# Chunked attention and two feed-forward layers: the attention products cut into 64x64 blocks, and the order of the opening changed

## The chip, the core and the metric

The kernel runs on one core of one Trainium2 chip. The metric is the device time of one execution in microseconds (us). The engines are named as the profile names them: PE (TensorE, matrix products), PEld (its weight loads), DVE (VectorE), ACT (ScalarE), POOL (GpSimd) and SP (SyncE, which only issues transfers here).

## What is computed

```python
# q, k, v: (4, 8, 576, 64); nine chunks of 64 positions for each head
scores = scale * np.matmul(q_c, k_c.transpose(0, 1, 2, 4, 3))     # 64x64 for each chunk and head
scores = scores - np.max(scores, axis=-1, keepdims=True)
attn = np.exp(scores)
attn = attn / (np.sum(attn, axis=-1, keepdims=True) + 1e-09)
out = np.matmul(attn, v_c)                                        # 64x64 for each chunk and head
...
x = out as (2304 tokens, 512)
h = x @ w_in;  r = np.maximum(h, 0.0);  x = (s * (r * r) + b) @ w_out      # 512 -> 2048 -> 512
...
P = exp(x @ w_gate - max), then 8 rounds of row and column scaling (8 experts)
out = sum over e of P[:, e:e+1] * (np.maximum(x @ w1[e], 0.0) @ w2[e])     # 512 -> 1024 -> 512
```

The weights w_in and w_out come as 64-bit floats and are turned into 32-bit numbers on the chip.

## The kernel before

The 2304 tokens are 18 token tiles of 128, that is, two chunks of 64 (c = 0, 1), and six groups `g` of three tiles. A tile `t` holds 8 heads as four pairs `p`; h or j is the head in its pair.

**Attention**, `attn_stages(t)`, is a generator of five stages. Stage 0 transposes q and k on PE into the banks pq and pk (L252, L258), and ACT copies them out: q into qT (L254), k into a block-diagonal tile kbd with zeros beside it (L261, two instructions of 64 partitions). Stage 1 makes the scores: for each pair and chunk one product of 128 rows with 64 weight columns (qT) and 128 moving columns (kbd) into the bank sc (L272); DVE takes the row maximum (L280) and subtracts it (L282). Stage 2 is the exponential on ACT (L285), the row sums on DVE (L287 to L289) and the division on POOL (L290). Stage 3 transposes the result into pa (L295) and ACT copies it to aT (L297). Stage 4 multiplies with v: one product for each pair and chunk, 128 weight columns from the block-diagonal tile vbd, 64 moving columns of aT, into the bank px (L303). ACT rounds px into xTh (L311), DVE writes the rest into xTl (L312). The zeros of kbd and vbd are written once, at the start, by DVE (L889) and POOL (L891). A product of 32-bit floats is two records each of weight load and matmul in the trace; a transpose and a product of split operands is one.

**Order.** Nothing is scheduled by a tool: each engine runs its instructions in the order in which the code records them, and waits at the head of its queue. `attention()` yields the stages of all tiles in a skewed order, and `stage(n)` runs the next n of these steps. One tile is four steps.

**The first feed-forward layer** goes over eight units `u` of 256 hidden columns. For a unit and a group, `up1` makes two banks ph of 12 matmuls each (L107 under `three`, both operands split in a high and a low part); ACT and DVE make the hidden tiles gh (L358, L360, L364), and `later()` makes their low part gl (L339, L344). `down1` makes four banks po of six matmuls each from gh and gl of both halves, and adds them to `xacc` (L389, L391). In unit 0 the steps of the attention lie between these (`side`). `down1` of a group is recorded after `up1` of the next one, through `prev`.

**Weights.** A unit's w_in and w_out are four blocks of 512 KB (raw). `convert` and `finish` make the high part wh and the low part wl of a block with ACT (L189, L190, L213), DVE (L191 to L197, L208) and POOL (L200, L201, L214); `unit_conversion` is a generator that does them one after the other, and `next(cg)` runs its next step. Blocks 0 and 1 are the two halves of w_in, 2 and 3 those of w_out.

**The experts.** The products of the second layer go through `up_chain` and `down_chain` (all PE work at L611), each on three or four of the PSUM banks that `kept["abc"]` names in turn. In the change from the last `up_chain` to the first `down_chain`, `prep_w2_first` splits the first w2 blocks: `w2_split` is an ACT instruction (L714) and a DVE one (L715), `w2_combine` a DVE subtraction (L718).

Of the kernel before, what the change touches and what calls it, by code (L numbers as in the profile page):

```python
# [25 lines left out]
def chunk_attention_ffn_moe(ctx, tc, q, k, v, w_in, w_out, s, b, w_gate, w1, w2, out):  # L26
# [52 lines left out]
    def accumulator(n, name):  # L79
# [4 lines left out]
    kbd = [  # L84
        cv.tile([P, NP, 2, 2, CH], F32, name="kbd"),
        cv.tile([P, NP, 2, 2, CH], F32, name="kbd1"),
    ]
    vbd = [cv.tile([P, NP, 2, 2, D], F32, name=f"vbd{i}") for i in range(2)]

    qk = {(nm, 0): at.tile([P, H, D], F32, name=f"{nm}0", bufs=1) for nm in "qk"}  # L90
    for i, key in enumerate((("q", 1), ("k", 1), ("q", 2), ("k", 2))):
        c0 = i % 2 * H * D
        qk[key] = spares[4 + i // 2][:, c0:c0 + H * D].rearrange("t (h d) -> t h d", h=H)
    prs = [at.tile([P, H, CH], F32, name="pr", bufs=1)]
    for i in (4, 5):
        prs.append(spares[i][:, 2 * H * CH:3 * H * CH].rearrange("x (h k) -> x h k", h=H))
# [30 lines left out]
    def load_v(t):  # L127
        for c in range(2):
            bb, s0 = divmod(t * P + c * CH, S)
            for j in range(2):  # L130
                nc.sync.dma_start(
                    out=vbd[t % 2][j * CH:(j + 1) * CH, :, c, j, :],
                    in_=v[bb, :, s0:s0 + CH, :].rearrange(
                        "(p two) s d -> two s p d", two=2
                    )[j],
                )
# [104 lines left out]
    def attn_stages(t):  # L241
# [4 lines left out]
        vb = vbd[t % 2]  # L246
        kb = kbd[t % 2]
# [11 lines left out]
        for j in range(2):  # L259
# [18 lines left out]
        sc3 = sc.rearrange("t (h k) -> t h k", h=H)  # L278
        mx = at.tile([P, H, 1], F32, tag="mx", name=f"mx{t}")
        nc.vector.tensor_reduce(out=mx, in_=sc3, axis=AX.X, op=ALU.max)  # L280
        pr = prs[t % 3]
        nc.vector.tensor_tensor(out=pr, in0=sc3, in1=mx.to_broadcast([P, H, CH]), op=ALU.subtract)  # L282
# [17 lines left out]
        px = bank(f"px{t}")  # L300
        for p in range(NP):
            for c in range(2):
                nc.tensor.matmul(  # L303
                    px[:, p * P + c * CH:p * P + (c + 1) * CH],
                    lhsT=vb[:, p, c].rearrange("x j d -> x (j d)"),
                    rhs=aT[:, p, c * CH:(c + 1) * CH],
                    start=True, stop=True,
                )
        px3 = px.rearrange("x (p t) -> x p t", p=NP)
        xh, xl = [x[:, :, o * P:(o + 1) * P] for x in xT[g]]  # L310
        nc.scalar.activation(out=xh, in_=px3, func=AF.Copy)  # L311
        nc.vector.tensor_tensor(out=xl, in0=px3, in1=xh.bitcast(F32), op=ALU.subtract)  # L312
        if t + 2 < NTT:
            load_v(t + 2)
# [413 lines left out]
    def prep_w2_first(room):  # L728
# [16 lines left out]
        for f, (b11, b22, b12, b21) in zip(HALVES, raw):  # L745
            w2_split(0, 0, b11, f)
            yield
            w2_split(0, 3, b21, f)
            w2_combine(b11, b11, b12)
            yield  # L750
            w2_split(0, 4, b22, f)
            w2_combine(b22, b22, b11)
            yield
            w2_split(0, 1, b22, f)
            yield
            w2_split(0, 2, b11, f)
            w2_combine(b21, b21, b11)
            w2late.extend([(0, 5, b12, f), (0, 6, b21, f)])
            yield
# [124 lines left out]
    with tc.manual_schedule():  # L884
# [3 lines left out]
        for z in kbd:  # L888
            nc.vector.memset(z, 0.0)  # L889
        for z in vbd:  # L890
            nc.gpsimd.memset(z, 0.0)  # L891
# [44 lines left out]
        for u in range(NU1):  # L936
# [9 lines left out]
            for g in range(NG):  # L946
# [10 lines left out]
                hs = up1(u, g, side if u else lambda: stage(3))  # L957
                if u == 0 and g == 0:
                    for _ in cg:
                        pass  # L960
                    plan_unit(1)
                    cg = unit_conversion(4)
                    next(cg)
                elif u == 0 or g:
                    next(cg, None)
# [187 lines left out]
```

## Time and profile before

| | |
|---|---|
| time, median of 3 runs | 1969.03 us (1967.58 to 1971.49) |
| the profiled execution's own time | 1969.52 us |
| its span, first to last instruction | 1967.7 us |
| PE busy | 1933.7 us (98% of the span) |
| DVE busy | 1374.4 us (70%) |
| ACT busy | 993.6 us (50%) |
| POOL busy | 158.1 us (8%) |
| mean granted clock of TensorE | 0.996 of full speed |

Busy time is the time in which an engine had an instruction under way. PE's instructions are pipelined and their ends are modelled, so a busy PE may still wait between two of them. A change can shorten the span only where it shortens what the last engine waits for at that place.

### The profile page before, as it was taken

Reading aid. Unit: us, or ns where it says so; the run is one execution under the profiler, and the core shown is the slowest. Engines: PE = TensorE matmul, PEld = TensorE weight load, DVE = VectorE, ACT = ScalarE, POOL = GpSimd, SP = SyncE. Lnnn points to the kernel's source line nnn. Section 1 sums busy time; section 2 is a strip of 40 time slices with the busy share of each in tenths; the row PEclk is TensorE's granted clock in tenths of the full one; section 3 lists DMA queues with packets and bytes.
Section 4 is the critical chain, followed back from the end, with each engine's and each line's share of the span. In section 5 each row is a group of like instructions: output and inputs, shape, how many; then the busy total and the mean of one; then the engine's idle time right before and its main releaser. Section 6 shows DMA issues by size and latency. Waiting matters only on the chain.

```text
span 1967.7 us, 33548 instructions
## 1 busy us (share of the span) xinstructions
PE 1933.7 (98%) x13283; PEld 1911.3 (97%) x13283; DVE 1374.4 (70%) x2365; ACT 993.6 (50%) x1793; POOL 158.1 (8%) x128
## 2 busy tenths in 40 slices
PE   7999999999899999999999999999999999999999
PEld 6899999999799999999999999999999999999998
DVE  5656777775767666656565656888887878788775
ACT  5664333335544445444444444555555555555553
POOL 4333333330000000000000000000000000000000
PEclk9999999999999999999999999999999999999999
DMA  8521111100155565556555656867676766767675
GB/s 201 133 65 44 44 43 43 43 22 11 39 201 213 196 228 219 208 202 227 218 210 202 225 218 232 287 184 225 177 229 188 223 201 208 220 190 227 180 228 167
DMA packets 295726, 335.64 MB, mean 171 GB/s; under 512 B 65937, under 2 KB 254353, under 8 KB 295569
## 3 DMA queue, kind: packets, MB, share of 16 engines
q1 hardware_dynamic: 295568, 333.50, 52.2%
q8 instruction: 104, 1.70, 0.3%
q14 instruction: 54, 0.43, 0.1%
HBM read 196.63 MB, written 136.84 MB: 169 GB/s over the span
## 4 chain that ended last, share of the span: by engine, by line
PE 92%; ACT 3%; DVE 3%; issue 1%; POOL 0%; DMA 0%; SPq 0%; DVEq 0%; ACTq 0%; POOLq 0%
PE wb L611 71%; PE po L107 10%; PE ph L107 9%; PE px L303 1%; PE sc L272 1%; ACT kbd L261 0%; ACT whole L659 0%; PE pa L295 0%; DVE x L520 0%; ACT r L368 0%; DMA raw<-in_moe_w_in_dram 0%; ACT r L358 0%; DVE sm L287 0%; DVE xs L523 0%; ACT qT L254 0%
## 5 line engine op out<-in xcount | busy, mean ns | idle before, releaser
L611 PE MATMUL wb<-x,x 128*128 128x256 f32 x6048 | 727.2, 283 | 2.3 <-DVE whole L665 1.4
L611 PEld LDWEIGHTS wb<-x,x 128*128 128x128 f32 x6048 | 726.3, 192 | 3.2 <-DVE whole L665 1.6
L611 PE MATMUL wb<-x,w1h 128*128 128x384 f32 x2688 | 687.8, 337 | 6.9 <-ACT wb L686 3.2
L611 PEld LDWEIGHTS wb<-x,w1h 128*128 128x128 f32 x2688 | 485.5, 188 | 9.8 <-ACT wb L686 4.2
L611 PE MATMUL wb<-x,w1l 128*128 128x384 f32 x1344 | 452.3, 337 | 0.1
L816 DVE TENSOR_TENSOR x<-st,x 128x1024 fp32r<-128x1024 f32 (+1 forms) x288 | 308.0, 1088 | 101.5 <-ACT x L815 100.5
L815 ACT ACTIVATE x<-st 128x1024 fp32r<-128x1024 f32 (+1 forms) x288 | 272.1, 945 | 109.6 <-issue 74.4
L611 PEld LDWEIGHTS wb<-x,w1l 128*128 128x128 f32 x1344 | 253.2, 188 | 0.4 <-DVE w1l L573 0.4
L843 DVE SCALAR_TENSOR_TENSOR whole<-wb,lg,whole 128x256 f32<-128x256 f32 (+1 forms) x333 | 165.9, 529 | 49.7 <-PE wb L611 47.2
L849 ACT ACTIVATE wb<-wb 128x256 f32<-128x256 f32 x216 | 79.4, 368 | 232.3 <-PE wb L611 221.7
L674 DVE SCALAR_TENSOR_TENSOR whole<-wb,whole 128x384 f32<-128x384 f32 x192 | 98.0, 552 | 126.9 <-PE wb L611 105.5
L659 ACT ACTIVATE whole<-whole 128x384 f32<-128x384 f32 x192 | 100.3, 527 | 157.1 <-DVE whole L665 119.4
L107 PE MATMUL po<-gh,wh 128*128 128x384 f32 x384 | 130.1, 339 | 0.0
L107 PE MATMUL ph<-xTh,wh 128*128 128x384 f32 x384 | 129.0, 336 | 0.7 <-ACT xTh L311 0.7
L107 PE MATMUL ph<-xTl,wh 128*128 128x384 f32 x384 | 128.4, 334 | 0.3 <-DVE xTl L312 0.3
L107 PE MATMUL po<-gh,wl 128*128 128x384 f32 x384 | 128.4, 334 | 0.0
L107 PE MATMUL po<-gl,wh 128*128 128x384 f32 x384 | 128.4, 334 | 0.0
L107 PE MATMUL ph<-xTh,wl 128*128 128x384 f32 x384 | 128.3, 334 | 0.0
L360 DVE SCALAR_TENSOR_TENSOR r<-r,s_bc 128x384 f32<-128x384 f32 x84 | 65.9, 785 | 70.7 <-ACT r L358 70.7
L573 DVE TENSOR_TENSOR w1l<-w,w1h 128x512 fp32r<-128x512 f32 (+1 forms) x128 | 78.9, 619 | 34.3 <-ACT w1h L571 34.3
L691 ACT ACTIVATE whole<-wb 128x384 f32<-128x384 f32 x96 | 47.4, 494 | 93.9 <-PE wb L611 93.8
L364 ACT ACTIVATE gh<-r,b_bc 128x384 fp32r<-128x384 f32 x84 | 51.8, 617 | 84.3 <-DVE r L360 84.3
(135 smaller groups left out, 2022.9 us busy)
## 6 DMA issues: line engine op xcount, KB each, us to landing
h<-whole SPq DMA_DIRECT2D x96, 1344.0 KB, 5.0
st<-h SPq DMA_DIRECT2D x216, 512.0 KB, 4.2
w<-in_moe_w_dram SPq DMA_DIRECT2D x60, 512.0 KB, 6.8
st<-h SPq DMA_DIRECT2D x72, 256.0 KB, 4.2
raw<-in_moe_w_in_dram SPq DMA_DIRECT2D x16, 512.0 KB, 3.7
raw<-in_moe_w_out_dram SPq DMA_DIRECT2D x14, 512.0 KB, 3.5
vbd<-in_v_dram SPq DMA_DIRECT2D x72, 64.0 KB, 2.5
out_dram<-whole SPq DMA_DIRECT2D x18, 256.0 KB, 3.3
```

Of the source, the lines that this page charges most:

```text
L107: nc.tensor.matmul(out, lhsT=x, rhs=y, start=(i == 0), stop=(i == n - 1))
L360: nc.vector.scalar_tensor_tensor(out=r, in0=r, scalar=s_bc[:, 0:1], in1=r, op0=ALU.mult, op1=ALU.mult)
L364: nc.scalar.activation(out=hh, in_=r, func=AF.Identity, bias=b_bc[:, 0:1])
L573: nc.vector.tensor_tensor(out=dst(lo), in0=src, in1=dst(hi).bitcast(F32), op=ALU.subtract)
L611: nc.tensor.matmul(out, lhsT=x, rhs=y, start=fresh and i == 0, stop=i == n - 1, skip_group_check=True)
L659: nc.scalar.activation(out=dst, in_=src, func=AF.Relu)
L674: nc.vector.scalar_tensor_tensor(out=dst, in0=view(b), scalar=0.0, in1=y, op0=ALU.max, op1=op)
L691: nc.scalar.activation(out=u2, in_=b, func=AF.Copy)
L815: nc.scalar.activation(out=h, in_=src, func=AF.Copy)
L816: nc.vector.tensor_tensor(out=l, in0=src, in1=h.bitcast(F32), op=ALU.subtract)
L843: nc.vector.scalar_tensor_tensor(out=dst, in0=src, scalar=g, in1=dst, op0=ALU.mult, op1=ALU.add)
L849: nc.scalar.activation(out=dst, in_=src, func=AF.Copy)
```

## The change

- **Blocks.** kbd and vbd and their zeros are gone. k is copied whole into kT by one ACT instruction; v is loaded into `vs` (three buffers instead of two, loaded three tiles ahead instead of two). Each product of a pair and chunk is now two products of 64 rows, 64 weight columns and 64 moving columns, one for each head; the scores go into two banks sc_0 and sc_1, and the output of stage 4 into two banks px_0 and px_1. `head(s, c)` sets which head goes where: two products that follow each other take different row halves and different column halves of the array. Maximum, subtraction, rounding and rest are done for each of the two banks, so they are twice as many instructions of half the size.
- **Unit 0.** `down1` of a group follows `up1` of the same group for groups 0 to 4; the steps of the attention between them are written out (`steps`, 12 to a group), and `next(cg)` is called within group 0.
- **Opening.** q, k of tiles 0 to 2 and v of tile 0 are loaded ahead of the first raw block, and the first `next(cg)` comes later in the opening loop.
- **Experts.** In `prep_w2_first` the split of b22 (slot 1) changes places with that of b11 (slot 2) and a combination. In `down_banks` banks 6 and 7 change places.
- The buffers for q, k and the exponentials leave the accumulator of group 4.

```diff
-    kbd = [
-        cv.tile([P, NP, 2, 2, CH], F32, name="kbd"),
-        cv.tile([P, NP, 2, 2, CH], F32, name="kbd1"),
-    ]
-    vbd = [cv.tile([P, NP, 2, 2, D], F32, name=f"vbd{i}") for i in range(2)]
+    vs = [cv.tile([P, NP, 2, D], F32, name=f"vs{i}") for i in range(3)]
+
+    def head(s, c):
+        return s if c == 0 else 1 - s
...
-        for j in range(2):
-            h = slice(j * D, (j + 1) * D)
-            nc.scalar.activation(
-                out=kb[h, :, :, j, :],
-                in_=pk[h].rearrange("x (p c t) -> x p c t", p=NP, c=2), func=AF.Copy,
-            )
+        kT = at.tile([P, NP, P], F32, tag="kT", name=f"kT{t}")
+        nc.scalar.activation(out=kT.rearrange("x p t -> x (p t)"), in_=pk, func=AF.Copy)
...
-        sc = bank(f"sc{t}")
+        sc = [bank(f"sc{t}_{s}")[:, :NP * CH] for s in range(2)]
         for p in range(NP):
-            for c in range(2):
-                nc.tensor.matmul(
-                    sc[c * CH:(c + 1) * CH, p * P:(p + 1) * P],
-                    lhsT=qT[:, p, c * CH:(c + 1) * CH],
-                    rhs=kb[:, p, c].rearrange("x j t -> x (j t)"),
-                    start=True, stop=True,
-                )
+            for s in range(2):
+                for c in range(2):
+                    h = slice(head(s, c) * D, (head(s, c) + 1) * D)
+                    k = slice(c * CH, (c + 1) * CH)
+                    nc.tensor.matmul(
+                        sc[s][k, p * CH:(p + 1) * CH], lhsT=qT[h, p, k], rhs=kT[h, p, k],
+                        start=True, stop=True,
+                    )
...
-        px = bank(f"px{t}")
+        px = [bank(f"px{t}_{c}")[:, :NP * CH] for c in range(2)]
         for p in range(NP):
             for c in range(2):
...
+                for s in range(2):
+                    r = slice(s * CH, (s + 1) * CH)
+                    nc.tensor.matmul(
+                        px[c][head(s, c) * D:(head(s, c) + 1) * D, p * CH:(p + 1) * CH],
+                        lhsT=vb[r, p, c, :], rhs=aT[r, p, c * CH:(c + 1) * CH],
+                        start=True, stop=True,
+                    )
+        for c in range(2):
+            px3 = px[c].rearrange("x (p t) -> x p t", p=NP)
...
-        kept["abc"] = itertools.cycle([(0, 2, 5, 6), (1, 3, 4, 7)])
+        kept["abc"] = itertools.cycle([(0, 2, 5, 7), (1, 3, 4, 6)])
...
-            w2_split(0, 1, b22, f)
-            yield
             w2_split(0, 2, b11, f)
             w2_combine(b21, b21, b11)
+            yield
+            w2_split(0, 1, b22, f)
...
         plan_unit(0)
-        load_raw(0)
         load_qk(1)
-        load_raw(1)
         load_v(0)
         load_qk(2)
+        load_raw(0)
+        load_v(1)
+        load_raw(1)
+        load_v(2)
         load_raw(2)
         load_raw(3)
-        load_v(1)
...
-            if i in (0,2,4,7,10,13,16,18):
+            if i in (4, 7, 8, 10, 11, 13):
...
+                    steps = iter((2, 1, 0, 2, 2, 2, 2, 1))
+
+                    def side():
+                        stage(next(steps, 2))
+                        if g == 0:
+                            next(cg, None)
+
+                hs = up1(u, g, side)
+                if u == 0 and g < NG - 1:
+                    stage(next(steps))
+                    later()
+                    stage(next(steps))
+                    down1(u, g, hs, side)
...
```

The change moves instructions at three places that matter below. The first is the start of ACT's queue. Before, the first two instructions work on a raw weight block:

```order
L189 ACTIVATE m_182<-raw_156 128x512
L190 ACTIVATE l_184<-raw_156 128x512
L254 ACTIVATE qT_199<-pq_194 128x512
L261 ACTIVATE kbd<-pk_201 64x8x64 x2
L254 ACTIVATE qT_215<-pq_210 128x512
L261 ACTIVATE kbd_109<-pk_217 64x8x64 x2
L189 ACTIVATE m_228<-raw_160 128x512
L190 ACTIVATE l_230<-raw_160 128x512
L285 ACTIVATE pr<-pr 128x512
```

Now ACT starts with q and k, and the first exponential stands ahead of both raw blocks:

```order
L251 ACTIVATE qT_191<-pq_186 128x512
L257 ACTIVATE kT_198<-pk_193 128x512
L251 ACTIVATE qT_207<-pq_202 128x512
L257 ACTIVATE kT_214<-pk_209 128x512
L282 ACTIVATE pr_115<-pr_115 128x512
L251 ACTIVATE qT_254<-pq_249 128x512
L257 ACTIVATE kT_261<-pk_256 128x512
L187 ACTIVATE m_265<-raw_162 128x512
L188 ACTIVATE l_267<-raw_162 128x512
L282 ACTIVATE pr_116<-pr_116 128x512
```

The weight work has moved behind three tiles' stage 0 and one exponential; nothing else stands ahead of it.

The second place is ACT's queue in unit 0 after the second hidden tile of group 0 (r_0_1 and gh_0_1; 0_1 is group 0, half 1). Before:

```order
L358 ACTIVATE r_0_1_548<-ph_0_1_533 128x384
L364 ACTIVATE gh_0_1_546<-r_0_1_548,b_bc 128x384
L297 ACTIVATE aT_558<-pa_553 128x512
L254 ACTIVATE qT_565<-pq_560 128x512
L261 ACTIVATE kbd_109<-pk_567 64x8x64 x2
L285 ACTIVATE whole<-whole 128x512
L213 ACTIVATE wh_154<-whole 128x512 x2
L297 ACTIVATE aT_611<-pa_606 128x512
L311 ACTIVATE xTh_349<-px_613 128x4x128
```

Now:

```order
L357 ACTIVATE r_0_1_623<-ph_0_1_608 128x384
L363 ACTIVATE gh_0_1_621<-r_0_1_623,b_bc 128x384
L282 ACTIVATE pr_116<-pr_116 128x512
L211 ACTIVATE wh_152<-whole 128x512
L294 ACTIVATE aT_666<-pa_661 128x512
L251 ACTIVATE qT_673<-pq_668 128x512
L257 ACTIVATE kT_680<-pk_675 128x512
L388 ACTIVATE whole<-po_0_0_684 128x384
L282 ACTIVATE whole<-whole 128x512
L294 ACTIVATE aT_726<-pa_721 128x512
L388 ACTIVATE whole<-po_0_1_728 128x384
```

The eviction of po of group 0 (L388) follows the hidden tile with five rows between them; before, the whole second group of attention tiles and `up1` of group 1 lay between.

The third place is DVE's queue near the end of the `up_chain` work, within `prep_w2_first` (x1_0 to x1_2 are the split operands, whole holds b11 to b21). Before:

```order
L715 TENSOR_TENSOR x1_2_5040<-whole_107,x1_0_5038 128x512
L718 TENSOR_TENSOR whole_107<-whole_107 128x512
L715 TENSOR_TENSOR x1_1_5039<-whole_107,x1_0_5038 128x512
L674 SCALAR_TENSOR_TENSOR whole_107<-wb2_5306,whole_107 128x3x128 x2
L676 TENSOR_TENSOR whole_107<-whole_107 128x3x128
L677 TENSOR_TENSOR whole_107<-whole_107 128x3x128
L715 TENSOR_TENSOR x1_2_5040<-whole_107,x1_0_5038 128x512
L718 TENSOR_TENSOR whole_107<-whole_107 128x512
```

Now:

```order
L714 TENSOR_TENSOR x1_2_5434<-whole_107,x1_0_5432 128x512
L717 TENSOR_TENSOR whole_107<-whole_107 128x512
L714 TENSOR_TENSOR x1_2_5434<-whole_107,x1_0_5432 128x512
L717 TENSOR_TENSOR whole_107<-whole_107 128x512
L673 SCALAR_TENSOR_TENSOR whole_107<-wb2_5700,whole_107 128x3x128 x2
L675 TENSOR_TENSOR whole_107<-whole_107 128x3x128
L676 TENSOR_TENSOR whole_107<-whole_107 128x3x128
L714 TENSOR_TENSOR x1_1_5433<-whole_107,x1_0_5432 128x512 x2
```

The split that follows the first combination is now of b11 (into x1_2), which that combination doesn't write; the split of b22 (into x1_1), which it writes, comes four instructions later.

## Rows read from the trace of the kernel before

**Rows 1.** The page: shares of the chain that ended last, by engine.

```profile
PE 92%; ACT 3%; DVE 3%; issue 1%; POOL 0%; DMA 0%; SPq 0%; DVEq 0%; ACTq 0%; POOLq 0%
```

**Rows 2.** By stretch: length, then PE, PEld, DVE, ACT, POOL busy; clock, DMA.

```profile
0.00:35.30 35.30, 23.38 (x173) 19.60 (x173) 19.43 (x36) 19.89 (x34) 18.28 (x26) 0.90 0.84 195
35.30:66.00 30.70, 27.20 (x217) 23.96 (x216) 17.56 (x36) 20.00 (x37) 10.17 (x10) 0.89 0.71 170
66.00:150.45 84.45, 83.43 (x674) 79.94 (x672) 52.27 (x94) 55.94 (x106) 26.11 (x22) 1.00 0.36 89
150.45:470.00 319.55, 319.55 (x1845) 319.55 (x1845) 221.58 (x392) 129.13 (x240) 103.54 (x72) 1.00 0.12 39
...
1220.00:1225.00 5.00, 5.00 (x22) 5.00 (x21) 3.65 (x8) 1.81 (x4) 0.00 (x0) 0.66 0.48 191
```

**Rows 3.** The chain that ended last, by time: start, us, what.

```profile
107.75 1.73 PE px L303 x16
109.48 0.44 PE pq L252 x4
...
110.36 1.02 PE sc L272 x16
111.38 1.25 PE po L107 x6
...
150.61 4.16 PE ph L107 x24
```

**Rows 4.** Groups of instructions, 35.3 to 150.44, with counts and mean ns.

```profile
L303 PE MATMUL px<-aT,vbd 128*128 128x64 f32 x240 | 29.1, 274 | 2.2 <-ACT aT L297 2.2
L107 PE MATMUL ph<-xTh,wh 128*128 128x384 f32 x48 | 16.8, 350 | 0.7 <-ACT xTh L311 0.7
L272 PE MATMUL sc<-kbd,qT 128*64 128x128 f32 x224 | 16.7, 295 | 0.0
...
L107 PE MATMUL po<-gh,wh 128*128 128x384 f32 x40 | 14.2, 356 | 0.0
...
L261 ACT ACTIVATE kbd<-pk 64x512 f32<-64x512 f32 x28 | 16.5, 588 | 0.3
L312 DVE TENSOR_TENSOR xTl<-px,xTh 128x512 fp32r<-128x512 f32 x15 | 10.3, 687 | 9.0 <-ACT xTh L311 9.0
L360 DVE SCALAR_TENSOR_TENSOR r<-r,s_bc 128x384 f32<-128x384 f32 x12 | 10.0, 831 | 18.1 <-ACT r L358 18.1
```

**Rows 5.** The page's groups: narrower instructions on PSUM banks.

```profile
L849 ACT ACTIVATE wb<-wb 128x256 f32<-128x256 f32 x216 | 79.4, 368 | 232.3 <-PE wb L611 221.7
L674 DVE SCALAR_TENSOR_TENSOR whole<-wb,whole 128x384 f32<-128x384 f32 x192 | 98.0, 552 | 126.9 <-PE wb L611 105.5
```

**Rows 6.** The opening by time, one engine after another: start, us, what.

```profile
7.22 0.66 ACT L189 ACTIVATE m<-raw 128x512 f32<-128x512 f32 x1 [5.21 <-DMA raw<-in_moe_w_in_dram]
...
9.44 1.27 POOL L200 TENSOR_TENSOR l<-l,e 128x512 f32<-128x512 f32 x1 [5.26 <-ACT kbd L261]
...
27.06 1.50 POOL L290 TENSOR_TENSOR whole<-whole,sm 128x512 f32<-128x512 f32 x1
...
5.11 1.12 PE L258 MATMUL pk<-ident,k 128*128 128x128 f32 x4
...
18.55 1.09 PE L295 MATMUL pa<-ident,pr 128*128 128x128 f32 x4 [2.83 <-POOL pr L290]
...
35.30 0.42 PE L107 MATMUL ph<-xTh,wh 128*128 128x384 f32 x1
```

**Rows 7.** From `up_chain` to `down_chain` by time, ACT and PE.

```profile
1218.38 0.63 ACT L714 ACTIVATE x<-whole 128x512 fp32r<-128x512 f32 x1 [1.49 <-DVE whole L718]
...
1219.44 0.62 PE L611 MATMUL wb<-x,w1h 128*128 128x384 f32 x2 [1.78 <-ACT wb L686]
1236.37 1.69 PE L611 MATMUL wb<-x,x 128*128 128x256 f32 x12 [1.36 <-DVE whole L665]
1242.45 3.77 PE L611 MATMUL wb<-x,x 128*128 128x256 f32 x28 [0.47 <-ACT wb L849]
```

More of the change, by code (lines that the diff above doesn't have):

```diff
@@ L83, in chunk_attention_ffn_moe @@
     spares = [accumulator(max(GT), f"spare{i}") for i in range(GT.count(max(GT)))]
-    kbd = [
-        cv.tile([P, NP, 2, 2, CH], F32, name="kbd"),
-        cv.tile([P, NP, 2, 2, CH], F32, name="kbd1"),
-    ]
-    vbd = [cv.tile([P, NP, 2, 2, D], F32, name=f"vbd{i}") for i in range(2)]
[L90 to L96, printed above, removed]
+    vs = [cv.tile([P, NP, 2, D], F32, name=f"vs{i}") for i in range(3)]
+    def head(s, c):
+        return s if c == 0 else 1 - s
+    qk = {(nm, i): at.tile([P, H, D], F32, name=f"{nm}{i}", bufs=1) for i in range(2) for nm in "qk"}
+    for i, nm in enumerate("qk"):
+        qk[nm, 2] = spares[5][:, i * H * D:(i + 1) * H * D].rearrange("t (h d) -> t h d", h=H)
+    prs = [at.tile([P, H, CH], F32, name=f"pr{i}", bufs=1) for i in range(2)]
+    prs.append(spares[5][:, 2 * H * CH:].rearrange("x (h k) -> x h k", h=H))
     def bank(name):
@@ L129, in load_v @@
             bb, s0 = divmod(t * P + c * CH, S)
-            for j in range(2):
+            for h in range(2):
                 nc.sync.dma_start(
-                    out=vbd[t % 2][j * CH:(j + 1) * CH, :, c, j, :],
+                    out=vs[t % 3][h * CH:(h + 1) * CH, :, c, :],
                     in_=v[bb, :, s0:s0 + CH, :].rearrange(
                         "(p two) s d -> two s p d", two=2
-                    )[j],
+                    )[head(h, c)],
                 )
@@ L245, in attn_stages @@
             xT[g] = new_x(g)
-        vb = vbd[t % 2]
-        kb = kbd[t % 2]
+        vb = vs[t % 3]
         a = qt.pop(t)
@@ L267, in attn_stages @@
         yield
-        sc = bank(f"sc{t}")
+        sc = [bank(f"sc{t}_{s}")[:, :NP * CH] for s in range(2)]
         for p in range(NP):
-            for c in range(2):
-                nc.tensor.matmul(
-                    sc[c * CH:(c + 1) * CH, p * P:(p + 1) * P],
-                    lhsT=qT[:, p, c * CH:(c + 1) * CH],
-                    rhs=kb[:, p, c].rearrange("x j t -> x (j t)"),
-                    start=True, stop=True,
-                )
-        sc3 = sc.rearrange("t (h k) -> t h k", h=H)
-        mx = at.tile([P, H, 1], F32, tag="mx", name=f"mx{t}")
-        nc.vector.tensor_reduce(out=mx, in_=sc3, axis=AX.X, op=ALU.max)
-        pr = prs[t % 3]
-        nc.vector.tensor_tensor(out=pr, in0=sc3, in1=mx.to_broadcast([P, H, CH]), op=ALU.subtract)
+            for s in range(2):
[6 more added lines that the diff above has]
+                    )
+        mx = at.tile([P, 2, NP, 1], F32, tag="mx", name=f"mx{t}")
+        pr = prs[t % 3]
+        for s in range(2):
+            sc3 = sc[s].rearrange("t (p k) -> t p k", p=NP)
+            nc.vector.tensor_reduce(out=mx[:, s], in_=sc3, axis=AX.X, op=ALU.max)
+            nc.vector.tensor_tensor(
+                out=pr[:, s::2], in0=sc3, in1=mx[:, s].to_broadcast([P, NP, CH]), op=ALU.subtract)
         yield
@@ L298, in attn_stages @@
         yield
-        px = bank(f"px{t}")
+        px = [bank(f"px{t}_{c}")[:, :NP * CH] for c in range(2)]
         for p in range(NP):
             for c in range(2):
[L303 to L314, printed above, removed]
+                for s in range(2):
+                    r = slice(s * CH, (s + 1) * CH)
[6 more added lines that the diff above has]
+            px3 = px[c].rearrange("x (p t) -> x p t", p=NP)
+            xh, xl = [x[:, :, o * P + c * CH:o * P + (c + 1) * CH] for x in xT[g]]
+            nc.scalar.activation(out=xh, in_=px3, func=AF.Copy)
+            nc.vector.tensor_tensor(out=xl, in0=px3, in1=xh.bitcast(F32), op=ALU.subtract)
+        if t + 3 < NTT:
+            load_v(t + 3)
         yield
@@ L956, in chunk_attention_ffn_moe @@
                     next(cg, None)
[L957 to L964, printed above, removed]
+                if u == 0:
+                    steps = iter((2, 1, 0, 2, 2, 2, 2, 1))
[9 more added lines that the diff above has]
+                    down1(u, g, hs, side)
+                    if g == 0:
+                        for _ in cg:
+                            pass
+                        plan_unit(1)
+                        cg = unit_conversion(4)
+                    else:
+                        next(cg, None)
+                    continue
+                if u == 0 or g:
                     next(cg, None)
```

5 lines of the change are left out of this document (removed).

## Prediction, made before the changed kernel was run

> **What bounds the kernel now.** I first read the chain of work that ended last: 92% of it is PE [rows 1]. The table of stretches shows where PE does not fill its time [rows 2]. From 150.45 us, where unit 1 begins, to 470 it is busy for the whole stretch; the change leaves that work alone, so what is won or lost before 150.45 moves it as a block. In the first 35.3 us PE is busy for 23.4, at a granted clock of 0.90 (part of the time at 1.2 instead of 2.4 GHz), and nobody else is full: this is a chain of dependent steps. From 35.3 to 66 it still has gaps, at a clock of 0.89. From 66 to 150.45 it is busy for 83.4 of 84.5: there PE's own work is the bound.
>
> How much of it is work? From 35.3 on the groups hold 48 matmuls of each of the three terms of ph and 40 of po [rows 4], 264 in all, at 4.16/24 = 0.173 us [rows 3]: 45.8 us. 240 records of px (15 tiles) at 1.73 us a tile are 26.0; 224 of sc (14 tiles) at 1.02 are 14.3; some 159 transposes (13 tiles' q and k, 15 tiles' pa, four to 0.44 us) are 17.5. Together 103.6 of 115.15 us. The other 11.5 are waits and the slow clock: 0.11 of 30.7, that is 3.4 us, is the clock.
>
> **The products in blocks.** A product of px is two records, 16 a tile in 1.73 us, 0.108 each; its 64 moving columns are half of those of a transpose, which takes 0.11 a record [rows 3]. So px is not held by the moving columns but by loading 128 weight columns. The records of sc have 64 weight columns and 128 moving ones, and 16 of them take 1.02: 0.064 each, or 0.128 for two. Their mean duration is 0.295, so they overlap; the two chunks of sc lie in different column halves. After the change a tile has 32 records in sc and 32 in px, each with half the weights of px and half the moving columns of sc: 0.054 to 0.064 each if nothing overlaps, which is 1.73 to 2.04 for 32. No record before uses half of the rows, so overlap between row halves isn't shown. The bounds are no overlap (about 1.9), two at a time as in sc (16 pairs at 0.064, 1.02) and four at a time (0.5). I take two at a time, since sc is the nearest row. Beside sc there is also a price for changing the tiling: six matmuls of po take 1.25 behind it instead of 6 x 0.173 = 1.04 [rows 3]. Now px changes it too; between nothing and these 0.2 I add 0.1, the middle.
>
> So sc stays at 1.02 and px goes from 1.73 to 1.12: 0.61 for each of the 15 tiles after 35.3 is **-9.2 us**. The three tiles before are in the chain of the opening.
>
> The Trainium skill (TensorEngine Tiling (Array Packing), Tiling Modes, Key Properties) says that the tiles load weights and multiply independently, which would give four at a time. Its section Restrictions and Gotchas speaks against that: different row tiles can't use the same PSUM bank at once. The two blocks that stand next to each other in one bank differ in their row half, so by that rule only neighbours from different banks would overlap, and two at a time is what remains. By the first the sum would be that of the rival with four at a time (1941), by the second it stays at 1949. No trace here has row tiles.
>
> **The instructions around them.** ACT loses one of two L261 (0.588) [rows 4] and has two xTh of 128x256 instead of one of 128x512, 2 x 0.37 [rows 5] for about 0.59: -0.44 a tile. DVE has three instructions in halves. From 0.552 for 384 columns [rows 5] and 0.687 for 512 [rows 4], about 0.42 for 256: 0.15 more for each, 0.45 a tile. In the stretch from 66 DVE was busy for 52.3 of 84.5 and ACT for 55.9 [rows 2]; with some ten tiles there they have 56.8 and 51.5, in about 70 us: 81% and 74%. I cost this at nothing, hidden behind PE. If PE's work fell to 57 us there, DVE would be the bound and all of it would show.
>
> **The opening.** ACT's first two rows wait 5.21 us for a raw block, until 7.22, and qT starts only behind them, some 1.1 later, though pk of tile 0 ended at 6.23 and pq before it [rows 6]. The weight work of two blocks stands ahead of the first maximum on DVE. POOL's first division lets PE's pa start at 18.55. After the change the first raw block comes behind three tiles' q and k and tile 0's v. I work it out from the durations that the same instructions have in this opening: qT and kT by 7.0, sc at the slow clock (about 2, as before) to 9, four DVE halves (1.6) to 10.6, exponential 0.63, sums 1.1, division 1.3: pa at 13.7 instead of 18.55, 4.9 earlier. From there to the first ph took 16.75 us. What moves into this stretch is the weight work: POOL now does the two products of both blocks (four at 1.27), one low part and two divisions before tile 2's pa, 8.6 us after 13.7, that is 22.3. Before, tile 2's division began at 27.06 and ph followed 8.2 later [rows 6], so ph could come at 29 or somewhat before. The first raw block lands late, at about 12, an estimate (seven loads of 0.26 MB ahead of its 0.52, at the stretch's 195 GB/s [rows 2]), when ACT asks for it after three tiles of q and k. I take 29.3 for 35.30: **-6 us**, between -3 (the raw blocks hold ACT) and -9.
>
> **Unit 0.** 24 matmuls of po, 4.2 us, move forward to group 0, into the stretch from 35.3 to 66 where PE waited. Against that, po now needs the hidden tiles just made: relu 0.5, L360 0.83, gh 0.6, low part 0.6 to 0.75, about 2.6 us after ph, and the queues of ACT and DVE. Between them PE has three steps of attention (about 0.9 each) and the first four matmuls of po (0.7): 3.4 us. That covers it in a quiet group. In group 0 the low part of w_out stands on POOL behind a division that waits for an exponential, some 3 us that are not covered. Of 11.5 us of loss I expect 9.5: **-2 us**, from +6 to -5. A group also takes 27 banks instead of 21 from eight; at 18 us a group a bank is asked for again after 5.3 us, longer than evictions of two instructions take.
>
> **Experts.** At 1219.44 PE had waited 1.78 us for L686, which stood on ACT behind a split that waited 1.49 for a combination [rows 7]. The exchanged split doesn't wait for it. After this wait the clock is 0.66 from 1220 to 1225 [rows 2], 1.7 us. Both gone, less a rest of 0.4: 3.1. The exchanged banks take away the wait of 1.36 for L665 at 1236.37, but ACT's queue is full to the wait at 1242.45, so PE would wait there instead: nothing. **-3 us**, between 0 and -5.
>
> **Sum.** -9.2 - 6 - 2 - 3 = -20.2 against the profiled execution's own 1969.5: 1949.3. The median is 0.5 lower than that execution, and I predict **1949 us**.
>
> **Rivals.** *Four blocks at a time* (chance 0.27): sc and px take 0.5 less, 14.5 us. From 66 on PE would need less than DVE's 57 us, so DVE holds about half of it: -8 more, 1941. For it: sc's columns already overlap. Against it: no row. The independent tiles of the Trainium skill's page TensorEngine Tiling (Array Packing) would come out here.
>
> *Waits in unit 0* (0.15): each of the five groups stalls 2 to 3 us at po or on banks, 10 to 15 us in all: 1959 to 1964. For it: DVE's L360 waited 18.1 us for ACT in 12 times [rows 4], so the way from ph to gh is slow. Against it: from 66 on PE waits for next to nothing with ACT and DVE at 66% and 62%.
>
> *No overlap of blocks* (0.10), the one on the other side: 32 records at 0.06 take 1.9 instead of 1.02 and, with 0.1, 2.0 instead of 1.73: 14 x 0.9 + 15 x 0.27 = +16.6 instead of -9.2. The sum is then +5.6: 1975, slower. It decides from 0.054 us a record up, where the other gains are used up.
>
> *The opening and the experts give nothing* (0.05): the raw blocks hold ACT as before, and DVE holds PE at 1236: about 1958. The remaining 0.03 is for anything worse.
>
> **How the numbers follow.** Two at a time, as forecast, has 0.40; with its terms' bounds it lies between 1943 and 1957. The range from 1936 to 1966 leaves out no overlap (0.10), the rest (0.03) and the best ends of four at a time (0.05). A difference of 0.2% (4 us) is about what a measurement of this kernel can tell from no change. Faster by more than that: 0.40 + 0.27 + 0.15 + 0.05, less 0.03 for stalls that eat all, 0.84. Within: 0.05. Slower: 0.11.
>
> **What would show it.** Right: 32 records of px in about 1.1 us and of sc in about 1.0, pa of tile 0 before 15 us, the first ph at 28 to 31, the first ph of unit 1 at 133 instead of 150.45, no wait of PE for L686 in the change to `down_chain` and a clock of 1.00 there. Wrong: blocks that start one after the other at 0.054 or more; waits of PE for gl or wl at the first po of a group; DVE above 95% from 66 on.

## The result, and the profile after

The changed kernel takes 1987.0 us (median of 4 runs, 1985.62 to 1988.73), beside 1968.64 (4 runs) for the kernel before: a ratio of 1.009 (95% interval 1.0072 to 1.0107). It is slower by 18.4 us. The prediction was 1949, between 1936 and 1966: the sign is wrong, and the time lies outside the range. The profiled execution took 1988.73.

The chain that ended last, in shares by engine, answers to [rows 1]: DMA and DVE have taken 2% from PE.

```profile
PE 90%; DVE 4%; ACT 3%; DMA 1%; issue 1%; SPq 0%; POOL 0%; DVEq 0%; ACTq 0%
```

Four stretches like those of [rows 2], cut where the first ph, the second group and unit 1 begin (length, then PE, PEld, DVE, ACT, POOL busy; clock, DMA). In the kernel before, the second group's first ph comes at 63.12, somewhat ahead of the cut at 66:

```profile
0.00:37.30 37.30, 20.53 (x285) 15.92 (x285) 19.59 (x45) 17.96 (x34) 16.73 (x24) 0.77 0.91 191
37.30:68.80 31.50, 24.14 (x354) 19.91 (x352) 16.89 (x42) 17.21 (x35) 8.14 (x8) 0.84 0.50 109
68.80:167.90 99.10, 80.76 (x996) 69.67 (x997) 54.83 (x129) 49.68 (x106) 27.65 (x23) 0.85 0.39 92
167.90:487.00 319.10, 317.66 (x1833) 317.34 (x1833) 223.48 (x396) 129.21 (x239) 103.69 (x72) 1.00 0.12 39
```

Unit 1 begins at 167.9 instead of 150.45, where the prediction had 133. So 17.4 us are lost before it, 2.0 of them by the first ph. In the third stretch PE is busy for 80.8 of 99.1 us, where it was 83.4 of 84.5, at a clock of 0.85 instead of 1.00. No other engine is near full (DVE 55%): what this stretch loses, it loses in waits and at a clock that is often at 1.2 GHz. What PE waited for up to 200 us (total, times, longest):

```profile
PE po L105 <- DVE gl L338: 10.4, 6, 2.9
PE px L302 <- ACT aT L294: 10.0, 3, 3.7
PE pq L249 <- DMA q<-in_q_dram: 6.8, 2, 4.2
PE po L105 <- ACT wh L211: 4.0, 1, 4.0
PE pa L292 <- POOL pr L287: 2.7, 3, 1.7
```

**The blocks did more than forecast.** In the chain that ended last, at full clock, 32 records of sc or px take 0.6 to 0.7 us, where 16 took 1.02 and 1.73 [rows 3]; the time until the last of 32 starts is 0.48. By the prediction's bounds (0.5 for four at a time, 1.02 for two) that is four at a time.

```profile
95.73 0.62 PE sc L269 x32
...
99.10 0.70 PE px L302 x32
```

**The loss in unit 0, seen by time.** These are rows of SP, ACT, DVE and PE around 120 us, group 3 of unit 0 (start, length, what; in brackets the idle time before):

```profile
119.81 0.54 SPq L175 DMA_DIRECT2D raw<-in_moe_w_out_dram  x1
...
119.25 0.64 ACT L211 ACTIVATE wh<-m 128x512 fp32r<-128x512 f32 x1 [1.50 <-DVE m L206]
124.28 0.69 ACT L187 ACTIVATE m<-raw 128x512 f32<-128x512 f32 x1 [4.40 <-DMA raw<-in_moe_w_out_dram]
...
132.28 0.61 ACT L363 ACTIVATE gh<-r,b_bc 128x384 fp32r<-128x384 f32 x1 [2.88 <-DVE r L359]
...
125.00 0.43 DVE L189 TENSOR_SCALAR m<-m 128x512 f32<-128x512 f32 x1 [5.79 <-ACT m L187]
...
125.95 0.68 PE L302 MATMUL px<-aT,vs 64*64 64x64 f32 x28 [0.59 <-ACT r L357]
128.07 0.66 PE L249 MATMUL pq<-ident,whole 128*128 128x128 f32 x4 [1.44 <-ACT qT L251]
...
132.82 0.69 PE L105 MATMUL po<-gl,wh 128*128 128x384 f32 x1 [2.69 <-DVE gl L338]
```

Read from the top: SP issues the load of a w_out block at 119.81. ACT asks for that block at 119.9, as its very next instruction, and stands for 4.40 us; DVE, whose weight work needs ACT's copy, stands for 5.79. The next stretches show both engines at zero and then PE short of work:

```profile
120.00:124.00 4.00, 4.00 (x55) 3.73 (x55) 0.00 (x0) 0.00 (x0) 1.24 (x1) 1.00 0.53 162
124.00:128.00 4.00, 2.04 (x40) 1.56 (x38) 1.81 (x4) 2.70 (x6) 1.48 (x1) 1.00 0.00 1
128.00:133.00 5.00, 2.25 (x10) 1.50 (x11) 3.65 (x10) 2.12 (x6) 2.32 (x3) 0.57 0.23 52
133.00:138.00 5.00, 5.00 (x46) 4.45 (x47) 3.32 (x9) 3.44 (x8) 0.83 (x1) 0.50 0.01 3
```

From 124 on, attention's copies, the hidden tiles and the weight work all stand in ACT's and DVE's queues, and PE waits 0.59, 1.44 and 2.69, the last time for gl, which po of the same group needs. Then PE is full again from 133 to 138, but at a clock of 0.50, the level that it has until 138.9. The same happens 26 us later: ACT waits 3.06 for the next block, PE 3.71 for aT.

```profile
128.70:138.90 10.20, 7.52 (x57) 5.84 (x59) 7.48 (x19) 4.90 (x12) 2.74 (x3) 0.50 0.09 21
...
150.12 0.68 ACT L187 ACTIVATE m<-raw 128x512 f32<-128x512 f32 x1 [3.06 <-DMA raw<-in_moe_w_out_dram]
...
154.44 1.13 PE L302 MATMUL px<-aT,vs 64*64 64x64 f32 x32 [3.71 <-ACT aT L294]
```

**Opening and experts.** The rows that answer to [rows 6] and [rows 7]:

```profile
14.85 0.65 PE L292 MATMUL pa<-ident,pr 128*128 128x128 f32 x4 [1.70 <-POOL pr L287]
...
14.49 0.68 ACT L187 ACTIVATE m<-raw 128x512 f32<-128x512 f32 x1 [1.11 <-DMA raw<-in_moe_w_in_dram]
...
25.04 1.10 DVE L206 SCALAR_TENSOR_TENSOR m<-raw,m 128x512 uint32<-128x512 uint32 x1
...
26.17 0.63 ACT L211 ACTIVATE wh<-m 128x512 fp32r<-128x512 f32 x1 [3.46 <-DVE m L206]
...
33.58 1.13 PE L302 MATMUL px<-aT,vs 64*64 64x64 f32 x32 [3.13 <-ACT aT L294]
...
37.27 0.42 PE L105 MATMUL ph<-xTh,wh 128*128 128x384 f32 x1
...
1238.52 0.61 PE L610 MATMUL wb<-x,w1h 128*128 128x384 f32 x2 [0.19 <-ACT wb L685]
...
1252.05 0.62 PE L610 MATMUL wb<-x,w1h 128*128 128x384 f32 x2 [2.25 <-ACT whole L690]
...
1250.56 1.06 ACT L814 ACTIVATE x<-st 128x1024 fp32r<-128x1024 f32 x1 [3.12 <-DMA st<-h]
```

The stretch at the change to `down_chain`, in the columns used above:

```profile
1236.00:1241.00 5.00, 4.81 (x28) 4.49 (x27) 3.85 (x8) 3.97 (x9) 0.00 (x0) 1.00 0.32 129
```

pa of tile 0 comes at 14.85 instead of 18.55, near the forecast 13.7, and yet ph at 37.3 instead of 35.30. At the change to `down_chain` the wait for L686 (now L685) is 0.19 instead of 1.78, and the clock from 1236 to 1241 is 1.00 instead of 0.66. The wait of 1.36 for L665 is gone too. But at 1252.05 PE waits 2.25 for ACT, which stands 3.12 for the first chunk of h, and 0.29, 0.35 and 0.71 at three places near by; before, the waits behind L686 were the 1.36 and 0.47 at 1242.45 [rows 7].

### The profile page after: what moved, and what is told of

The parts are those of the page before. It is cut to its first block, busy times and chain, and to the rows that moved or that the text cites. A ratio compares the mean times of both kernels' runs of the same rounds, so it can differ in the third digit from the quotient of the medians.

```text
span 1986.9 us, 34732 instructions
## 1 busy us (share of the span) xinstructions
PE 1925.5 (97%) x13859; PEld 1893.1 (95%) x13859; DVE 1378.9 (69%) x2417; ACT 983.8 (50%) x1793; POOL 156.2 (8%) x126
## 4 chain that ended last, share of the span: by engine, by line
PE 90%; DVE 4%; ACT 3%; DMA 1%; issue 1%; SPq 0%; POOL 0%; DVEq 0%; ACTq 0%
PE wb L610 70%; PE po L105 10%; PE ph L105 9%; DMA raw<-in_moe_w_out_dram 0%; DVE r L359 0%; DMA st<-h 0%; DVE sm L284 0%; ACT whole L658 0%; DVE mx L277 0%; PE px L302 0%; DMA raw<-in_moe_w_in_dram 0%; DVE x L519 0%; PE sc L269 0%; ACT r L357 0%; ACT r L367 0%
## 5 line engine op out<-in xcount | busy, mean ns | idle before, releaser
L105 PE MATMUL po<-gl,wh 128*128 128x384 f32 x384 | 132.7, 346 | 10.4 <-DVE gl L338 10.4
L105 PE MATMUL po<-gh,wh 128*128 128x384 f32 x384 | 134.5, 350 | 4.3 <-ACT wh L211 4.0
```

The costliest lines, as they stand in the source:

```text
L105: nc.tensor.matmul(out, lhsT=x, rhs=y, start=(i == 0), stop=(i == n - 1))
```

## The experiments

All times are medians. The difference is taken to the kernel before, run on the same chip (1969.05, 1970.56, 1970.63 and 1968.41 in four sets). "Unit 1" is the start of its first ph in the profile, that is, in one execution. The ratio is not that of the two medians and can differ from the difference by 1 to 2 us, for "wh later" in sign too. All these kernels compute the whole result.

| kernel | us | difference | ratio (95%) | unit 1 |
|---|---|---|---|---|
| blocks alone | 1965.01 | -4.0 | 0.9975 (0.9964 to 0.9985) | 143.4 |
| order of unit 0 alone | 1997.10 | +28.1 | 1.0141 (1.0126 to 1.0156) | 177.6 |
| opening alone | 1973.85 | +4.8 | 1.0026 (1.0016 to 1.0035) | 154.4 |
| experts alone | 1968.08 | -1.0 | 0.9996 (0.9987 to 1.0006) | 148.4 |
| after, unit 0 of before | 1965.10 | -5.5 | 0.9972 (0.9961 to 0.9983) | 146.7 |
| after, raw block earlier | 1971.68 | +1.1 | 1.0004 (0.9995 to 1.0013) | 149.7 |
| after, po one group later | 1978.36 | +7.8 | 1.0038 (1.0026 to 1.0049) | 158.9 |
| after, three steps everywhere | 1994.97 | +24.4 | 1.0115 (1.0099 to 1.0130) | 173.6 |
| raw earlier, opening of before | 1969.82 | -0.8 | 0.9989 (0.9978 to 0.9999) | 147.8 |
| raw earlier, wh later in the opening | 1972.30 | +1.7 | 0.9999 (0.9989 to 1.0009) | 152.9 |
| blocks and experts | 1962.13 | -8.5 | 0.9951 (0.9933 to 0.9969) | 144.6 |
| blocks, undivided instructions | 1980.78 | +10.2 | 1.0043 (1.0026 to 1.0061) | 142.4 |
| unit 0 alone, raw earlier | 1980.94 | +12.5 | 1.0058 (1.0041 to 1.0075) | 162.3 |
| raw earlier and po later | 1967.22 | -1.2 | 0.9993 (0.9984 to 1.0003) | 148.9 |

**The four parts alone.** Each takes the kernel before and one part of the diff shown above: the blocks with `vs` and the halved instructions; the order of unit 0 (for groups 0 to 3, since group 4's accumulator still holds buffers of the attention); the loads and the numbers of the opening loop; the exchanged split and banks.

> The kernel before with the 64x64 blocks alone (kT, vs, two banks each for the scores and for the output; one more load of v at the start); unit 0, the opening's order and the experts as before. Theory A (the order of unit 0 costs the time: the first po behind its own ph waits for gl, PE stands, the clock falls to 1.2 GHz): this alone is faster than before, between 5 and 15 us, since sc and px take 0.6 to 0.7 us a tile instead of 1.02 and 1.73. Theory B (the blocks cost: less PE work between waits, so the clock falls more often, and twice as many DVE instructions): slower than before by 5 us or more.

> The kernel before with the new order of unit 0 alone, for groups 0 to 3 (group 4's accumulator still holds buffers of the attention, so it stays behind the next group). Theory A: slower than before by 8 to 20 us, with waits of PE for gl at the first po of each group and for the raw blocks on ACT, and a granted clock well below 1.00 from 35 to 150 us. Theory B: within 4 us of before.

> The kernel before with the new order of the first loads and the later weight steps of the opening alone. The trace after shows the first raw block landing at 14.5 instead of 7.2 us and the first ph at 37.3 instead of 35.3, though the first exponential is 3.4 us earlier. Theory A: this alone costs 0 to 3 us. Theory C (the opening costs the time: the weights of w_out come later, and everything behind them): slower by 8 us or more.

> The kernel before with the exchanged w2 split and the exchanged banks 6 and 7 alone. The trace after gains 3.2 us at the wait for L686 and gives 1.75 back some 8 us later, where ACT waits for the first h chunks to land. Expected by all theories: 1 to 2 us faster, which is near what three rounds can tell from nothing.

Unit 0 is the loss, the opening a smaller one, the blocks gain, and the experts can't be told from nothing. Theory A has the signs, but not the sizes: the blocks gave 4.0 where 5 to 15 was expected, unit 0 cost 28.1 for 8 to 20, the opening 4.8 for 0 to 3. The parts don't add up either: alone they sum to +27.9, together they cost 18.4. With the blocks alone, the stretch from group 1 to unit 1 and 15 us within it read:

```profile
60.60:143.40 82.80, 73.83 (x1021) 66.70 (x1022) 59.67 (x134) 51.52 (x112) 27.99 (x23) 0.98 0.40 97
100.00:115.00 15.00, 11.95 (x234) 10.37 (x235) 13.94 (x39) 11.02 (x26) 6.90 (x6) 0.89 0.22 50
```

PE has lost its lead: it is idle for 9 of 82.8 us, and in the second row DVE is busy for 93%. PE's waits from 33 to 200 us add up to 16.6 us in 14 entries, most of them for xTl, aT, the subtraction and the division, where before they were 4.6. In the order of unit 0 alone the waits are few and large. These are PE's three largest from 33 to 200 us, and one of ACT's:

```profile
PE po L107 <- DVE gl L339: 9.6, 4, 4.3
PE ph L107 <- ACT xTh L311: 4.5, 4, 2.4
PE po L107 <- ACT wh L213: 3.8, 1, 3.8
...
ACT m L189 <- DMA raw<-in_moe_w_out_dram: 6.9, 2, 3.7
```

**What in unit 0.** The first of four runs puts unit 0 back whole. The second moves one step of the weight work ahead of po, so that the 24 matmuls of po and their steps lie between the load of a block and ACT's use of it:

```diff
                     stage(next(steps))
+                    if g:
+                        next(cg, None)
                     down1(u, g, hs, side)
...
-                    else:
-                        next(cg, None)
```

The third leaves that and records po one group later (`down1(*prev, side)`), as before. The fourth gives each place three steps, `stage(3)`, so 18 steps to a group. Between the second ph and po there are three steps in both; but `later()`, which records the second gl, now stands behind all three, where it stood behind the first.

> The changed kernel with unit 0 as before (po one group behind, three steps of the attention at every place). If the order of unit 0 is what costs (theory A), this undoes it: the parts measured alone leave -4 for the blocks, +5 for the opening and -1 for the experts, so about 1968 to 1970, level with before. If blocks and opening hurt each other (rival), it stays above 1978.

> The changed kernel, in which the last weight step of a group stands ahead of the group's down1 and not behind it, so that a raw block is asked for half a group before ACT needs it. In the trace after, ACT waits 4.4 and 3.1 us for raw blocks of w_out. If these stalls make gl late and PE stand (rival D), this gives 6 to 10 us back: 1977 to 1981. If they are hidden behind other lateness, as they must be in the kernel before, where ACT waits 5.8 us for the same blocks without cost, less than 3 us: 1984 to 1988.

> The changed kernel with only one thing of unit 0 undone: down1 works on the group before (for group 0 its four places hold the attention steps alone). The 12 steps a group stay. If the waits for gl behind the own ph are the cause (theory A1), this gives most of the 18 us back: 1970 to 1975. If the cause is that 12 steps a group keep the attention just in time, so that everything waits for it (theory A2), it stays at 1982 to 1988.

> The changed kernel with the other half of unit 0 undone: three steps of the attention at every place, as before, so that it runs ahead of the groups; po stays behind its own ph. Theory A1: 1983 to 1990, since gl is as late as ever. Theory A2: most of the 18 us come back, 1970 to 1975.

The order of unit 0 costs 18.4 + 5.5 = 23.9 us in the changed kernel. Moving one weight step, which changes no instruction, gives 17.3 back, more than either expectation (1971.68, where 1977 to 1981 was the better one). The 5.8 us of ACT's waits in the kernel before, which the expectation names, lie at 169.6 and 179.7, in unit 1, where PE is busy all the time; in its unit 0 there are none. In the kernel with the moved step ACT no longer waits for a raw block between the first ph and unit 1. One load is issued at 124.45, and ACT takes the block at 133.40, without a wait (rows of SP and ACT, then two stretches and PE's largest wait from 33 to 200 us):

```profile
124.45 0.35 SPq L175 DMA_DIRECT2D raw<-in_moe_w_out_dram  x1
...
133.40 0.67 ACT L187 ACTIVATE m<-raw 128x512 f32<-128x512 f32 x1
...
38.00:68.40 30.40, 23.02 (x354) 19.05 (x352) 16.92 (x42) 17.00 (x35) 7.94 (x7) 0.89 0.50 111
68.40:149.70 81.30, 71.05 (x996) 61.33 (x997) 53.55 (x129) 49.68 (x107) 27.30 (x23) 0.98 0.47 112
...
PE po L105 <- DVE gl L338: 8.6, 7, 2.2
```

The clock of the last stretch is 0.98 instead of 0.85.

But the late raw block is not all that the moved step mends. At the end of group 1 and the start of group 2 it had put two `convert` steps, of two blocks of w_in, right behind each other: ACT then stands 3.38 us for POOL, with relu behind it. These are ACT's row and group 2 in the changed kernel, and group 2 with the step moved:

```profile
96.81 0.67 ACT L188 ACTIVATE l<-raw 128x512 f32<-128x512 uint32 x1 [3.38 <-POOL m L199]
...
91.80:117.80 26.00, 20.89 (x276) 17.69 (x276) 17.04 (x38) 14.29 (x30) 8.36 (x7) 0.87 0.40 88
```

```profile
90.90:110.90 20.00, 18.00 (x277) 15.28 (x277) 13.55 (x35) 13.55 (x30) 7.24 (x6) 1.00 0.54 128
```

Group 2 holds no wait for a raw block, and yet 6.0 us of the gain lie there. Groups 3 and 4, which held the two waits, take 11.3 less (50.1 and 38.8 us from the first ph of group 3 to unit 1).

Po one group later gives 10.6 of the 23.9 back, so the position of po alone explains less than half of the loss; at 1978.36 it lies in neither of the expected ranges. ACT still waits 6.8 us for raw blocks in that kernel, and PE pays less for it, since po has another group's gl. With three steps everywhere it is 6.0 slower, beyond both ranges: PE then waits 13.0 us for gl and 7.9 for wh (10.4 and 4.0 before that edit). Nothing came back of what theory A2 expected. But the edit gives each group more attention and also records gl later in DVE's queue; which of the two makes it slower, this run doesn't show, so by itself it doesn't refute A2.

```profile
PE po L105 <- DVE gl L338: 13.0, 6, 4.0
PE po L105 <- ACT wh L211: 7.9, 2, 5.1
```

**The opening, and what blocks can give.** Two runs start from "raw earlier": one with the opening loop and load order of before, one with the later numbers `(4, 7, 9, 11, 12, 13)`, which put wh behind aT in ACT's queue. Two more start from the blocks alone: one adds the experts and the moved buffers; the other gives sc and px tiles of two banks, so that DVE and ACT need one instruction for both:

```diff
-    ps = [open_pool(ffn_banks, "ps", bufs=8, space=PSUM)]
+    ps = [open_pool(ffn_banks, "ps", bufs=4, space=PSUM)]
+    ps2 = open_pool(ffn_banks, "ps2", bufs=2, space=PSUM)
...
+        nc.vector.tensor_reduce(out=mx, in_=sc4, axis=AX.X, op=ALU.max)
```

> The kernel of the run with the weight step ahead of down1 (1971.7 us), with the opening of before (order of the first loads and places of the weight steps). The opening alone cost 5 us on the kernel before. If it costs the same here: 1965 to 1968. If the opening and the new order of unit 0 belong together (rival): 1970 to 1974.

> The same kernel (weight step ahead of down1) with the new order of the loads, but the two finishes of w_in one attention step later, so that aT of tiles 1 and 2 stands ahead of them on ACT. In the trace after, ACT waits 3.5 and 2.3 us for the weight chain with aT queued behind, and PE waits for aT with it. If this queue is what makes the opening slow, not the later landing of the raw blocks: 2 to 6 us faster than 1971.7. If the landing is the cause: within 2 us of it.

> The blocks and the exchange in the experts, with unit 0 and the opening of before. By the parts (-4 and -1) about 1964 to 1965 against 1969 to 1970 of before. It would be the fastest so far.

> The kernel before with the blocks alone (-4 us), but the two banks of the scores and of the output are one tile of two banks each, so that maximum, subtraction, rounding and rest are one instruction each again; the other work has four banks to itself instead of a share of eight. The blocks take 0.48 us a product, yet unit 1 began only 7 us earlier. If the halved DVE instructions (0.45 us a tile on DVE) hold the gain: 3 to 8 us faster than the blocks alone. If the chain of dependent steps holds it, not DVE's time: within 2 us. If four banks are too few: slower than the blocks alone.

The opening costs 1.9 us beside "raw earlier" (1969.82, between the two expected ranges), 3.0 between the kernels "after, unit 0 of before" and "blocks and experts", and 4.8 alone. With wh later, the first ph comes at 36.0 instead of 38.0, but nothing is left of it at unit 1 (152.9 for 149.7). The time is within 2 us of "raw earlier", which the expectation takes for the late landing as the cause; the landing alone was not tested. The blocks and the experts without the two other parts beat both kernels, at 1962.13. That is 8.5 us, where the two alone sum to 5.0; the moved buffers are in it too, and why it is more stays open. From there to the changed kernel the steps are 3.0 for the opening and 23.9 for unit 0.

The undivided instructions bring unit 1 only 1.0 us forward (142.4 for 143.4), less than single runs of one kernel differ (1963.35 to 1966.95 for the blocks alone). So no gain of the undivided instructions is left at unit 1, though DVE is at 93% in places; but all other work has four banks instead of eight there too, and what that costs before unit 1 isn't separated. The kernel as a whole is slower in units 1 to 7, where ph and po have only those four banks. Its row and its largest wait, and then the row of the blocks alone:

```profile
142.40:530.00 387.60, 370.18 (x2112) 358.61 (x2110) 258.83 (x455) 161.89 (x294) 103.71 (x72) 1.00 0.11 33
...
PE ph L107 <- DVE whole L393: 12.8, 13, 1.8
```

```profile
143.40:512.20 368.80, 364.72 (x2112) 357.67 (x2111) 258.34 (x454) 160.90 (x294) 103.63 (x72) 1.00 0.11 35
```

**Do the two mends of unit 0 add up?** One run has the weight step moved in "unit 0 alone", one has both mends in the changed kernel.

> The kernel before with the new order of unit 0 alone (groups 0 to 3; 1997.1 us), and the weight step ahead of down1 as in the run that gave 15 us back. If the raw block that is asked for too late is the main cost of the new order (theory D), this gives 12 us or more back here too: below 1985. If po behind its own ph is the main cost (A1), less than 6 us: above 1991.

> The changed kernel with both mends of unit 0: the weight step ahead of down1 (-15 alone) and po one group behind (-9 alone), the 12 steps a group and all else as changed. If the two mends act on the same wait (ACT stands for a raw block, so gl is late, so po stands): 1968 to 1972, no better than the first alone. If they are separate: 1960 to 1965.

In unit 0 alone the moved step gives back 15.6 of 28.1. In the changed kernel both mends give 19.6, while alone they give 17.3 and 10.6: they largely mend the same wait, since a late raw block does harm through the gl that po waits for. The 4.3 us that still lie between this kernel and the one with unit 0 of before are not explained. The largest single wait is one of 4.74 in group 0, but from the first ph to that of the second group the two kernels take the same time (25.9 and 25.6 us), so it can't be that wait; 2.2 of the 4.3 are there at unit 1 (148.9 for 146.7):

```profile
52.30 1.11 PE L292 MATMUL pa<-ident,pr 128*128 128x128 f32 x4 [4.74 <-POOL pr L287]
```

## Why the prediction was wrong

**The step that failed is "Unit 0": -2 us, from +6 to -5.** It measured +23.9 in the changed kernel. Three things were wrong in it.

1. I counted the instructions that po needs and compared 2.6 us with 3.4 us of cover. I did not follow what `next(cg)` does at its new place. It stands at the end of a group, and the next group begins with another. One issues the load of a block, the other starts with the ACT instruction that needs that block; before, `up1` with its six steps lay between, and ACT had no wait for a raw block from 35 to 150 us. So the load lies open: 4.40 and 3.06 us of waiting at ACT, with DVE behind it. One group earlier the same pair of steps are two `convert` steps, and ACT stands 3.38 us for POOL between them. None of these waits was in the sum or the rivals. Parting the steps gave 17.3 us; in the profiles 6.0 lie in the group with the two `convert` steps and 11.3 in the groups with the open loads.
2. "That covers it in a quiet group" was too kind even without that wait. With the raw block early PE still waits for gl in seven places, 8.6 us, and 4.0 for wh in group 0. I had named some 3 us in group 0, but for the low part on POOL: PE waits 0.3 for that, and the 4.0 are for the high part on ACT.
3. I priced the waits at their length. After them PE works at 1.2 GHz. An estimate from the clock of 0.84 and 0.85 in the two stretches of unit 0: with half the speed for the time concerned, 0.16 x 31.5 x 2 + 0.15 x 99.1 x 2 = 40 us at that level, where before it was 0.11 x 30.7 x 2 = 7. With the raw block early it is 10. How much of the 17.3 us is the waits and how much the clock, no run separates.

The rival "waits in unit 0" had the right place, and a loss there where I had a gain: five groups with 2 to 3 us each. It was given 10 to 15 us; unit 0 cost 23.9.

**Blocks, -9.2.** The mechanism is right and its size wrong on both sides. The records run four at a time, and so the rival was right on that; but the gain is 4.0 alone, not the 17 to which the rival's 8 more would have brought it. The rival let DVE hold half of its gain, because PE would need less than DVE's 57 us from 66 on; that reading was wrong, for 83.4 less 1.6 us for each of some ten tiles is 67. What "blocks alone" shows is a ring of small waits (16.6 us) on DVE, ACT and POOL; that they hold the gain is read from there and not tested, and joining DVE's halves, with fewer banks, did not free it. The 0.1 us for changing the tiling had no ground either: six matmuls of po take 1.13 us until the next record starts behind transposes (86.32) as behind px (82.74), and 1.16 behind sc (74.17), so all but 0.03 of what they take above 1.04 comes without a change of the tiling. The Trainium skill (TensorEngine Tiling (Array Packing), Tiling Modes, Key Properties) says that tiles work independently; 32 records in 0.62 us agree. The rule of its section Restrictions and Gotchas, that different row tiles can't share a bank at once, would have left two at a time here; the measurement decides: at 0.62 us for 32, where two at a time would take 1.02, two blocks of one bank, in different partitions, must have overlapped.

**Opening, -6.** The way to pa was right (14.85 for 13.7). The step "from there on POOL's work puts tile 2's pa at 22.3" failed: that pa came at 28.7. The first raw block reaches ACT at 14.49 (I had estimated 12; before, it was 7.22), so its weight work meets the softmax of tiles 1 and 2 on DVE: `m` (L206) comes only at 25.04, wh at 26.17, and aT of tile 1 stands behind it on ACT. The second block's wh does the same to aT of tile 2, for which PE waits 3.13 at 33.58. Moving wh behind aT brought ph 2.0 us forward and no time in the end, so why the 2 to 5 us are lost is only partly shown.

**Experts, -3.** The wait and the clock went as forecast, 1.6 + 1.7 us. The waits that followed, the one behind the h chunks above all, add up to 3.6 instead of 1.8 us, so 1.8 went back. I named what stands in ACT's queue there but not the transfer behind it. What remains, 1.5, is below what the run with this part alone could show (-1.0, interval across 1).

**The signs and the sums.** Of the signs named, pa before 15, the clock of 1.00 and, but for 0.19 us, the vanished wait for L686 came true; px and sc were faster than named, the first ph and unit 1 later. "Waits of PE for gl or wl at the first po of a group" is the sign that showed the forecast wrong. DVE stayed far below 95% (55% in the third stretch). The spread "between 1943 and 1957" was too narrow for its own terms: their lower and upper bounds taken together give about 1941 and 1963.

## What to carry to other kernels

Where a generator's steps are moved, write down what stands between the step that issues a load and the step that uses it: an edit that adds no instruction can bring the two together, and in a queue that runs in order everything behind the user waits for the transfer (4.40 us on ACT here, 5.79 on DVE). A consumer placed right behind its producer needs its cover counted in the queues of all engines on the way, with whatever else those hold, not in PE's instructions. And a part that frees an engine which was just the bound is worth what the next chain leaves: measure the parts one by one, since here one of four outweighed all that the others gained.

## What the runs showed that was not expected

- 32 records (16 products) of 64x64 blocks take 0.62 us for sc and 0.70 for px at full clock, against 1.02 and 1.73 for 16 larger records that do the same work.
- With short waits of PE came the half clock, for longer than they lasted: 0.59, 1.44 and 2.69 us of waiting between 125 and 133 us, and 10.2 us (128.7 to 138.9, the last wait in it) at 0.50.
- In the opening the half clock cost nothing. Two kernels with the same opening show it:

```profile
0.00:38.00 38.00, 21.48 (x285) 16.83 (x285) 19.57 (x45) 18.20 (x34) 16.92 (x25) 0.78 0.88 189
```

```profile
0.00:38.10 38.10, 22.84 (x284) 17.91 (x285) 19.58 (x45) 18.17 (x34) 17.30 (x25) 1.00 0.88 191
```

  The first is "raw earlier", the second "po one group later": 0.78 and 1.00, and the first ph at the same time (38.0 and 38.1); PE is busy for 21.5 and 22.8 of the 38 us and does not set the pace there.
